# Row 1's statistics ahead of row 0's low halves, kernel halves ahead of signal halves, and the last two convolution rows one by one

## The chip, the core and the metric

One core of a Trainium2 chip runs the whole program. The metric is device time in microseconds, the median of repeated executions. The kernel before takes 1179.39 us, the median of three runs from 1178.54 to 1179.56. Names of engines: PE is TensorE (PEld its weight loads), DVE is VectorE, ACT is ScalarE, POOL is GpSimd, SP is SyncE, which issues most loads. ACT and POOL issue some transfers too.

## The reference, cut to what matters

Four sublayers are computed on x (2048 positions, 576 channels), each with a layer norm in front and a residual sum behind: a Fourier mixing, a gated long convolution, and both again with the same weights.

```python
def _A_ref(x, dft_seq_re, dft_seq_im, dft_hid_re, dft_hid_im):
    a = jnp.einsum("bsd,ed->bse", x, dft_hid_re)
    b = jnp.einsum("bsd,ed->bse", x, dft_hid_im)
    return jnp.einsum("ts,bse->bte", dft_seq_re, a) - jnp.einsum("ts,bse->bte", dft_seq_im, b)

def _B_ref(q, k, v, shift_k, ssm_k, ssm_D):
    k_shift = sum(k_pad[:, t:t + S, :] * shift_k[:, 3 - t] for t in range(4))
    kv = k_shift * v
    y = irfft(rfft(kv, 2S) * rfft(ssm_k, 2S))[:S] + kv * ssm_D     # per channel
    return q * y

x = x + _A_ref(_layernorm(x), ...)
x = x + _B_ref(_layernorm(x), k, v, ...)
x = x + _A_ref(_layernorm(x), ...)
x = x + _B_ref(_layernorm(x), k, v, ...)
```

The signal kv and the kernel ssm_k of the long convolution do not depend on x, so the kernel computes that convolution once and uses it in both gated sublayers.

## The kernel before, in words

**Rows.** Positions are laid out as 128 partitions by 16 rows (J = 16). A row is a 128 x 576 block. Every matrix that PE multiplies is split into a high part, rounded by a copy on ACT (`AF.Copy` into fp32r), and a low part, the difference, taken by DVE. A product is three matmuls: high by high, high by low, low by high. Line 101 is the rounding and line 102 the difference of the general helper `split`.

**The first Fourier sublayer** (`layer`) takes 128 steps, 16 rows for each of two matrices (g) and four column blocks (tb). A step loads a 128 x 512 tile of the sequence matrix (`load_c`, line 171 through SP), splits it (lines 101 and 102, tile `mats<-flts`), and runs 14 matmuls of 512 columns into the accumulators s and rm. In the first 16 steps the row itself must also be made: `load_x`, statistics (`norm_stats`, lines 185 to 187 on DVE, then a power on POOL in line 188), a bias on DVE (194), the normalizing copy on ACT (195), its rounding on ACT (199) and the low halves on DVE (201 for the last 64 channels, 202 for the first 512). From row 8 on the statistics are sums on ACT (652, 654).

**The convolution's branch** (`branch`) is a generator that the steps of `layer` advance in halves, so its work lies between the steps. Its first Fourier stage takes 32 items from the list `todo`: for each row j a kernel half (`src` 1, ssm_k) and a signal half (`src` 0). `f1_loads` keeps three landings ahead. `f1_split` multiplies a signal row with the loaded v (line 430), then rounds (101) and subtracts (102) into tile f1r. `f1_products` issues the small matmuls (PE `bf<-f1r`, six in a visit), copies the two banks out on ACT (455) and stores them (456). Three banks take turns. For the first four rows all kernel halves come first, then the signal halves, and each has its own products of 288 columns; from row 4 on the two halves of a row share a tile pair, and three visits of 384 columns follow when both are there.

**The short convolution** (`convolve`) makes k_shift for the signal rows, two rows at a time: four multiplications (line 397) and three additions (402) of 128 x 1152 elements for each pair on DVE, 56 in all. They are handed out evenly between the halves of the list so that a pair is ready when its first signal half is due (`later`, `left`).

**What sets the order.** The code issues the instructions in one order with priorities; a scheduler places them on each engine's queue, and each engine runs its queue in that order. `behind(...)` (line 105 on) and `tc.issue_after` tell the scheduler to place an instruction no earlier than another one. The stage after this one needs all of `todo` done; it begins at about step 45.

Of the kernel before, what the change touches and what calls it, by code (L numbers as in the profile page):

```python
# [13 lines left out]
OP = mybir.AluOpType  # L14
# [4 lines left out]
D = 576  # L19
J = S // P  # L20
# [5 lines left out]
EPS = 1e-5  # L26
# [5 lines left out]
K_FIRST = 4  # L32
# [22 lines left out]
KR = 4  # L55
# [13 lines left out]
def fnet_h3_kernel(ctx: ExitStack, tc: tile.TileContext, x, c_mat, w_re, w_im, k_pad, v, shift_k,  # L69
                   ssm_k, ssm_d, f1c, i2c, midc, out):  # L70
    nc = tc.nc
# [28 lines left out]
    def split(h, l, src):  # L100
        a = nc.scalar.activation(h, src, AF.Copy).ins  # L101
        return a, nc.vector.tensor_tensor(l, src, h.bitcast(F32), OP.subtract).ins  # L102

    @contextmanager
    def behind(*instructions):
        with ExitStack() as stack:
            for i in instructions:
                stack.enter_context(tc.issue_after(i))
            yield
# [36 lines left out]
    def two(v):  # L146
        return v.rearrange("p (a n) -> p a n", a=2)
# [16 lines left out]

    anchor, made, rounded, pows, biased, halved, added, evac, parted, stored = [], [], [], [], [], [], [], [], [], []

    scaled, asked = [], []

    def load_after(dst, src):
        with tc.issue_after(anchor[-1]):  # L170
# [10 lines left out]
    def norm_stats(src):  # L181
        m = ring["stat"]()
        st, mv, ve, rs = m[:, :12].rearrange("p (a c) -> p a c", a=2), m[:, 12:14], m[:, 14:15], m[:, 15:16]
        for i in range(2):
            nc.vector.bn_stats(st[:, i, :], src[:, i * HD:(i + 1) * HD])
        nc.vector.bn_aggr(mv, st)
        nc.vector.tensor_scalar(ve, mv[:, 1:2], EPS, None, op0=OP.add)  # L187
        pows.append(nc.gpsimd.tensor_tensor(rs, ve, mhalf, OP.pow).ins)  # L188
        return mv, rs, m[:, 16:17]

    def normed(src, y):
        mv, rs, nb = norm_stats(src)
        yield
        biased.append(nc.vector.tensor_scalar(nb, mv[:, 0:1], rs, -1.0, op0=OP.mult, op1=OP.mult).ins)
        scaled.append(nc.scalar.activation(y, src, AF.Identity, bias=nb, scale=rs).ins)

    def to_x(y, j):
        t = xs[:, j, :]
        rounded.append(nc.scalar.activation(t[:, :D], y, AF.Copy).ins)
        h = t.bitcast(F32)  # L200
        nc.vector.tensor_tensor(t[:, D:D + REM], y[:, NC * P:], h[:, NC * P:D], OP.subtract)
        made.append(nc.vector.tensor_tensor(t[:, D + REM:], y[:, :NC * P], h[:, :NC * P], OP.subtract).ins)
        return t

    t_d = dr.tile([P, 2 * J, 2 * D], F32, name="td")
    v_d = [dr.tile([P, 2 * J, HD], F32, name=f"vd{h}") for h in range(2)]
# [7 lines left out]
    X = [None] * J  # L214
# [131 lines left out]
    def parts(i):  # L346
        v = ring[i]()
        return v[:, :D], v[:, D:]
# [4 lines left out]
    def branch():  # L353
# [3 lines left out]
        at = lay(flts, SC_AT + CRAW * NT, ("so", D, 4), ("land", D, 3))  # L357
# [15 lines left out]

        def load_k(upto):
            while k_loaded[0] < min(upto, (J + 4) // 2):
                i = k_loaded[0]
                at = i % KR * 2 * D
                nc.sync.dma_start(ks[:, at:at + 2 * D], k_pad[:, 2 * i * D:2 * (i + 1) * D])
                k_loaded[0] += 1

        def k_rows(row):

            at = row % (2 * KR) * D
            if at + 2 * D <= KR * 2 * D:
                return [(slice(0, 2), two(ks[:, at:at + 2 * D]))]
            return [(slice(n, n + 1), ks[:, o:o + D].unsqueeze(1)) for n, o in ((0, at), (1, 0))]

        def convolve():
            for i in range(J // 2):
                if not wt:  # L390
                    load_w4()
                load_k(i + KR - 1)
                rp = rows[i] = two(ring["rp"]())
                for t in range(4):
                    out_t = two(tmp) if t else rp
                    for n, k in k_rows(2 * i + t):
                        nc.vector.tensor_tensor(out_t[:, n], k, wt[3 - t][:, n], OP.mult)  # L397
                    yield
                    if t == 1:
                        load_k(i + KR)  # L400
                    if t:
                        nc.vector.tensor_tensor(rp, rp, out_t, OP.add)  # L402
                        yield

        todo = [(1, 1), (0, 1)] + [(j, 1) for j in range(2, K_FIRST)] + [(j, 0) for j in range(K_FIRST)]
        todo += [(j, src) for j in range(K_FIRST, J) for src in range(2)]
        loads = [0]

        def f1_loads(upto):
# [16 lines left out]
        def f1_split(j, src):  # L426
            r = landed.pop((j, src))
            if not src:
                row = rows[j // 2][:, j % 2, :]
                nc.vector.tensor_tensor(row, row, r, OP.mult)  # L430
                r = row
            elif j == 0:
                nc.vector.tensor_tensor(r[:1], r[:1], tmp[:1, D:], OP.add)
            if j < K_FIRST:
                xf = parts("xf")
                parted[:] = split(xf[0], xf[1], r)
                return xf
            if not src:
                t = ring["xp"]()
                paired[:] = t[:, :2 * D], t[:, 2 * D:]  # L440
            h, l = (t.rearrange("p (a s d) -> p a s d", a=2, s=2)[:, :, src, :] for t in paired)
            parted[:] = split(h, l, two(r))
            return tuple(paired)
# [14 lines left out]
        conv, made_ops, visits = convolve(), 0, []  # L458
        def visit(half):
            if visits and visits[0][0] <= half:  # L460
                f1_products(*visits.pop(0)[1:])

        for n, (j, src) in enumerate(todo):
            f1_loads(n + 1)
            if n < 2:
                yield
            xf = f1_split(j, src)
            if j < K_FIRST:
                visits += [(2 * n + 2, j, fcs[j], xf, hf * HD, HD, "so", hf * D + src * HD) for hf in range(2)]
            elif src:  # L470
                visits += [(2 * n + 3, j, fcs[j], xf, at, VW, "sp", at) for at in range(0, 2 * D, VW)]
            if n:
                f1_loads(n + 3)
            later = [m for m in range(n + 1, len(todo)) if todo[m][1] == 0 and 7 * (todo[m][0] // 2 + 1) > made_ops]
            for half in range(2):
                visit(2 * n + half)
                if later and n > 2:
                    left = 7 * (todo[later[0]][0] // 2 + 1) - made_ops
                    for _ in range(-(-left // (2 * (later[0] - n) - half)) if left > 0 else 0):
                        next(conv)  # L480
                        made_ops += 1
                yield
# [6 lines left out]
        at = lay(m1, 0, ("df", 2 * D, 3), ("mc", 4 * P, 1))  # L489
# [284 lines left out]
    with tc.issue_after(biased[0]):  # L774
        next(br)
        with behind(*parted, scaled[0]):
            load_c((0, 0, 0))
        load_x(1)
        with behind(rounded[0]):
            load_c((0, 0, 1))  # L780
        load_x(2)
    used = 4
# [17 lines left out]
    for n, whole in layer(get_x0, lambda j: x[:, j, :], done0, pending):  # L800
        part = whole == "part"
        if part:
            whole = False
        if (whole or whole is not None and n % J < J - 1) and n <= F1_END and not part:
            at = n if whole else n - 0.5
# [27 lines left out]
        m = n - PREP  # L833
# [207 lines left out]
    for n, whole in layer(get_x1, lambda j: xb_d[j], done1, pending, 1):  # L1041
# [143 lines left out]
```

## Time and profile before

| what | value |
|---|---|
| median of three runs | 1179.39 us |
| the profiled execution's own time | 1178.94 us |
| its span, first to last instruction | 1177.0 us |
| granted PE clock, mean | 0.999 |
| DVE busy over the span | 867.8 us (74%) |
| ACT busy over the span | 647.8 us (55%) |
| POOL busy over the span | 75.7 us (6%) |

The profile records one execution. The span leaves 1.94 us of its time outside. Busy is the time in which at least one instruction of an engine runs; ends of matmuls are modelled, so a short wait of PE can lie hidden in its busy time. A row of the timeline gives start, duration, engine, line, operation and tiles, and in brackets how long the engine was idle before it and what ended that. SPq, ACTq and POOLq are rows in which an engine's queue issues a transfer.

### The profile page before, as it was taken

Reading aid. Unit: us, or ns where it says so; the run is one execution under the profiler, and the core shown is the slowest. Engines: PE = TensorE matmul, PEld = TensorE weight load, DVE = VectorE, ACT = ScalarE, POOL = GpSimd, SP = SyncE. Lnnn points to the kernel's source line nnn. Section 1 sums busy time; section 2 is a strip of 40 time slices with the busy share of each in tenths; the row PEclk is TensorE's granted clock in tenths of the full one; section 3 lists DMA queues with packets and bytes.
Section 4 is the critical chain, followed back from the end, with each engine's and each line's share of the span. In section 5 each row is a group of like instructions: output and inputs, shape, how many; then the busy total and the mean of one; then the engine's idle time right before and its main releaser. Section 6 shows DMA issues by size and latency. Waiting matters only on the chain.

```text
span 1177.0 us, 18134 instructions
## 1 busy us (share of the span) xinstructions
PE 1165.9 (99%) x6198; PEld 989.8 (84%) x6198; DVE 867.8 (74%) x1564; ACT 647.8 (55%) x1280; POOL 75.7 (6%) x115
## 2 busy tenths in 40 slices
PE   9999999999999999999999999999999999999997
PEld 6776667988899988898888898888888888889997
DVE  7899984688787788877757666866685777774674
ACT  8865655567766667766645667434434445450210
POOL 2310000000000000001101111000000000001111
PEclk9999999999999999999999999999999999999999
DMA  9879898546766766749966777772762877894531
GB/s 326 298 232 306 270 300 284 164 139 178 214 206 192 210 181 191 193 135 258 272 197 216 249 245 239 239 238 89 251 240 73 251 262 257 265 332 149 194 111 41
DMA packets 147453, 255.64 MB, mean 217 GB/s; under 512 B 16161, under 2 KB 56353, under 8 KB 147362
## 3 DMA queue, kind: packets, MB, share of 16 engines
q1 hardware_dynamic: 111890, 210.17, 56.6%
q10 hardware_dynamic: 28560, 37.91, 9.1%
q0 software_dynamic: 6912, 6.43, 2.4%
q8 instruction: 48, 0.79, 0.3%
q14 instruction: 43, 0.35, 0.1%
HBM read 187.80 MB, written 66.65 MB: 216 GB/s over the span
## 4 chain that ended last, share of the span: by engine, by line
PE 93%; DVE 2%; DMA 2%; ACT 1%; issue 1%; SPq 0%; POOL 0%; DVEq 0%; ACTq 0%
PE s L78 54%; PE bk L78 31%; PE rm L78 6%; PE bf L78 2%; DMA t<-ud 1%; DVE f1f L397 1%; DMA vd<-flts 0%; DVE f1f L402 0%; DVE mats L102 0%; DMA early<-in_x 0%; ACT flts L516 0%; DMA flts<-vd 0%; DMA td<-flts 0%; DVE f1r L102 0%; ACT mid L516 0%
## 5 line engine op out<-in xcount | busy, mean ns | idle before, releaser
L78 PE MATMUL s<-mats 128*128 128x512 f32 x2102 | 548.0, 396 | 2.7 <-DVE mats L762 1.5
L78 PEld LDWEIGHTS s<-mats 128*128 128x128 f32 x2102 | 382.7, 189 | 83.8 <-issue 10.9
L102 DVE TENSOR_TENSOR mats<-flts,mats 128x512 fp32r<-128x512 f32 x206 | 140.9, 688 | 55.8 <-ACT mats L101 53.4
L101 ACT ACTIVATE mats<-flts 128x512 fp32r<-128x512 f32 x206 | 128.2, 628 | 79.9 <-PE bk L78 29.6
L516 ACT ACTIVATE flts<-bk 128x288 f32<-128x288 f32 (+1 forms) x192 | 78.4, 409 | 97.7 <-PE bk L78 85.2
L78 PE MATMUL bk<-mid 128*128 128x288 f32 x704 | 127.9, 298 | 0.7 <-DVE mid L522 0.4
L78 PEld LDWEIGHTS bk<-mid 128*128 128x128 f32 x704 | 111.2, 188 | 19.7 <-ACT flts L516 4.5
L78 PE MATMUL bk<-w,u 128*128 128x288 f32 x864 | 120.5, 295 | 0.2
L78 PEld LDWEIGHTS bk<-w,u 128*128 128x128 f32 x864 | 116.8, 188 | 2.4 <-ACT flts L516 1.4
L522 DVE TENSOR_TENSOR mid<-flts,mid 128x576 fp32r<-128x576 f32 (+1 forms) x149 | 92.5, 625 | 7.4 <-ACT mid L516 5.3
L78 PE MATMUL rm<-mats 128*128 128x512 f32 x304 | 94.7, 391 | 0.0
L516 ACT ACTIVATE mid<-flts 128x576 fp32r<-128x576 f32 (+1 forms) x148 | 79.5, 574 | 1.9 <-DMA flts<-vd 0.9
L78 PE MATMUL bk<-mats 128*128 128x288 f32 (+1 forms) x376 | 67.8, 317 | 0.0
L78 PEld LDWEIGHTS rm<-mats 128*128 128x128 f32 x304 | 56.9, 188 | 12.5 <-issue 0.3
L455 ACT ACTIVATE flts<-bf 128x384 f32<-128x384 f32 (+1 forms) x104 | 43.2, 462 | 42.9 <-PE bf L78 40.5
L291 DVE TENSOR_TENSOR flts<-flts,bk 128x288 f32<-128x288 f32 x48 | 21.8, 454 | 60.6 <-PE bk L78 58.3
L78 PE MATMUL s<-t,mats 128*128 128x512 f32 x264 | 65.3, 390 | 0.3 <-DVE t L102 0.3
L188 POOL TENSOR_TENSOR flts<-flts 128x1 f32<-128x1 f32 x34 | 28.0, 824 | 517.0 <-DVE flts L187 517.0
L78 PE MATMUL bk<-mats,t 128*128 128x288 f32 (+1 forms) x368 | 59.3, 303 | 0.0
L78 PEld LDWEIGHTS s<-t,mats 128*128 128x128 f32 x264 | 49.4, 188 | 11.2 <-DVE t L102 0.8
L516 ACT ACTIVATE flts<-flts 64x288 f32<-64x288 f32 x128 | 56.7, 443 | 3.9
L78 PEld LDWEIGHTS bk<-mats 128*128 128x128 f32 x376 | 55.6, 188 | 3.4
(152 smaller groups left out, 1496.6 us busy)
## 6 DMA issues: line engine op xcount, KB each, us to landing
flts<-in_c_mat SPq DMA_DIRECT2D x148, 256.0 KB, 3.5
ph<-in_c_mat SPq DMA_DIRECT2D x54, 512.0 KB, 4.4
flts<-in_c_mat SPq DMA_DIRECT2D x30, 512.0 KB, 5.2
flts<-td SPq DMA_DIRECT2D x53, 288.0 KB, 3.1
td<-flts ACTq DMA_DIRECT2D x36, 384.0 KB, 4.5
vd<-flts ACTq DMA_DIRECT2D x64, 144.0 KB, 3.1
flts<-vd SPq DMA_DIRECT2D x32, 288.0 KB, 4.1
ud<-ph ACTq DMA_DIRECT2D x12, 512.0 KB, 6.4
```

The lines of the kernel that those rows point to most:

```text
L78: return nc.tensor.matmul(ps, lhsT, rhs, start=first, stop=last, skip_group_check=more).ins
L101: a = nc.scalar.activation(h, src, AF.Copy).ins
L102: return a, nc.vector.tensor_tensor(l, src, h.bitcast(F32), OP.subtract).ins
L188: pows.append(nc.gpsimd.tensor_tensor(rs, ve, mhalf, OP.pow).ins)
L291: added[:] = [nc.vector.tensor_tensor(r[:, cs], r[:, cs], ps[:, :HD], OP.add).ins]
L397: nc.vector.tensor_tensor(out_t[:, n], k, wt[3 - t][:, n], OP.mult)
L455: stored[:] = [nc.scalar.activation(so[:, i, :], ps[i], AF.Copy).ins]
L516: last_act.append(nc.scalar.activation(*args, **kw).ins)
L522: nc.vector.tensor_tensor(l, src, h.bitcast(F32), OP.subtract)
```

## The change

Four edits, all in the first 200 us of the program.

1. `to_x` leaves the low halves of row 0 to a new function `low_x`. The start now issues row 1's statistics (`stats0(1)`) first and puts `low_x` of row 0 behind row 1's line 187 (`joined`). The second tile of the sequence matrix is placed behind row 0's low halves as well.
2. The second item of `todo`, the kernel half of row 0, is split behind the last rounding (`rounded[-1:]`), which at that place is row 1's.
3. From row 4 on the list takes the kernel half (1) before the signal half (0). The tile pair is taken at the kernel half, the visits follow the signal half, and the deadlines of the short convolution move with it by one item.
4. The last pair of the short convolution is made one row at a time: 7 operations of 128 x 576 for row 14, then 7 for row 15, each row with its own deadline (`conv_ops`).

```diff
@@ to_x
         rounded.append(nc.scalar.activation(t[:, :D], y, AF.Copy).ins)
+        if j > 0 or X[0] is not None:
+            low_x(y, t)
+        return t
+
+    def low_x(y, t):
         h = t.bitcast(F32)
         nc.vector.tensor_tensor(t[:, D:D + REM], y[:, NC * P:], h[:, NC * P:D], OP.subtract)
         made.append(nc.vector.tensor_tensor(t[:, D + REM:], y[:, :NC * P], h[:, :NC * P], OP.subtract).ins)
-        return t
...
+        def k_row(row, part):
+            at = (row + part.start) % (2 * KR) * D
+            return [(part, ks[:, at:at + D].unsqueeze(1))]
+
@@ convolve
+                for part in (slice(0, 2),) if i < J // 2 - 1 else (slice(0, 1), slice(1, 2)):
...
+        def conv_ops(j):
+            return 7 * (j // 2 + 1) if j < J - 2 else 7 * (J // 2 + j - J + 2)
+
-        todo += [(j, src) for j in range(K_FIRST, J) for src in range(2)]
+        todo += [(j, src) for j in range(K_FIRST, J) for src in (1, 0)]
@@ f1_split
-                parted[:] = split(xf[0], xf[1], r)
+                with behind(*rounded[-1:] if (j, src) == todo[1] else ()):
+                    parted[:] = split(xf[0], xf[1], r)
                 return xf
-            if not src:
+            if src:
                 t = ring["xp"]()
...
-            elif src:
+            elif not src:
                 visits += [(2 * n + 3, j, fcs[j], xf, at, VW, "sp", at) for at in range(0, 2 * D, VW)]
@@ start
         load_x(1)
-        with behind(rounded[0]):
+        stats0(1)
+        with behind(joined[-1]):
+            low_x(LN[0][0], X[0])
+        with behind(rounded[0], made[0]):
             load_c((0, 0, 1))
         load_x(2)
```

Line numbers shift: 195 and 199 stay, 201 and 202 become 206 and 207, 397 and 402 become 406 and 411, 430 becomes 442, 433 becomes 445, 455 and 456 become 468 and 469.

**Start, DVE.** The rows from the low half of the first sequence tile (102) on. flts holds the statistics, early the x rows. Before:

```order
L102 TENSOR_TENSOR mats<-flts,mats 128x512
L201 TENSOR_TENSOR mats<-early,mats 128x64
L202 TENSOR_TENSOR mats<-early,mats 128x512
L102 TENSOR_TENSOR mats<-flts,mats 128x512
L186 BN_AGGR flts<-flts 128x2
L185 BN_STATS flts<-early 128x6
L187 TENSOR_SCALAR flts<-flts 128x1
L433 TENSOR_TENSOR flts<-flts,f1f 1x576
L186 BN_AGGR flts<-flts 128x2
L194 TENSOR_SCALAR flts<-flts 128x1
```

And of the change:

```order
L102 TENSOR_TENSOR mats<-flts,mats 128x512
L186 BN_AGGR flts<-flts 128x2
L185 BN_STATS flts<-early 128x6
L187 TENSOR_SCALAR flts<-flts 128x1
L206 TENSOR_TENSOR mats<-early,mats 128x64
L207 TENSOR_TENSOR mats<-early,mats 128x512
L102 TENSOR_TENSOR mats<-flts,mats 128x512
L186 BN_AGGR flts<-flts 128x2
L194 TENSOR_SCALAR flts<-flts 128x1
```

Row 1's 186 and 187 moved ahead of row 0's low halves and of the second tile's low half; the addition of ssm_d (433, now 445) moved behind row 1's bias (194).

**Start, ACT.** The rows that lead to row 1's rounding (199), from the copies out of the first product's banks on. Before:

```order
L455 ACTIVATE flts<-bf_66 128x288
L455 ACTIVATE flts<-bf_67 128x288
L101 ACTIVATE f1r<-flts 128x576
L456 DMA td<-flts 256x1x288
L455 ACTIVATE flts<-bf_68 128x288
L455 ACTIVATE flts<-bf_66 128x288
L195 ACTIVATE early<-early,flts 128x576
L101 ACTIVATE f1r<-flts 128x576
L199 ACTIVATE mats<-early 128x576
L101 ACTIVATE mats<-flts 128x512
```

And of the change:

```order
L468 ACTIVATE flts<-bf_66 128x288
L468 ACTIVATE flts<-bf_67 128x288
L469 DMA td<-flts 256x1x288
L468 ACTIVATE flts<-bf_68 128x288
L468 ACTIVATE flts<-bf_66 128x288
L195 ACTIVATE early<-early,flts 128x576
L101 ACTIVATE mats<-flts 128x512
L199 ACTIVATE mats<-early 128x576
L101 ACTIVATE f1r<-flts 128x576
```

The kernel halves (f1r) no longer stand in front of row 1; the third sequence tile's rounding (mats<-flts) moved in front of row 1's rounding.

**Between the steps, ACT.** A piece of the queue at about step 27 of the first sublayer; f1r<-f1f is the rounding of a signal half, f1r<-flts that of a kernel half. Before:

```order
L455 ACTIVATE flts<-bf_66 128x384
L101 ACTIVATE f1r<-f1f 128x2x288
L455 ACTIVATE flts<-bf_68 128x384
L101 ACTIVATE mats<-flts 128x512
L456 DMA td<-flts 256x1x384
L455 ACTIVATE flts<-bf_67 128x384
L455 ACTIVATE flts<-bf_68 128x384
```

And of the change:

```order
L468 ACTIVATE flts<-bf_66 128x384
L468 ACTIVATE flts<-bf_68 128x384
L101 ACTIVATE mats<-flts 128x512
L101 ACTIVATE f1r<-f1f 128x2x288
L469 DMA td<-flts 256x1x384
L468 ACTIVATE flts<-bf_67 128x384
L468 ACTIVATE flts<-bf_68 128x384
```

The signal's rounding, which waits for DVE's line 430 (now 442), stood between the two copies that empty a visit's banks; now it stands behind both.

More of the change, by code (lines that the diff above doesn't have):

```diff
@@ L165, in fnet_h3_kernel @@
     anchor, made, rounded, pows, biased, halved, added, evac, parted, stored = [], [], [], [], [], [], [], [], [], []
-    scaled, asked = [], []
+    scaled, asked, joined = [], [], []
     def load_after(dst, src):
@@ L186, in norm_stats @@
         nc.vector.bn_aggr(mv, st)
-        nc.vector.tensor_scalar(ve, mv[:, 1:2], EPS, None, op0=OP.add)
+        joined.append(nc.vector.tensor_scalar(ve, mv[:, 1:2], EPS, None, op0=OP.add).ins)
         pows.append(nc.gpsimd.tensor_tensor(rs, ve, mhalf, OP.pow).ins)
@@ L393, in convolve @@
                 rp = rows[i] = two(ring["rp"]())
[L394 to L402, printed above, removed]
-                        yield
+                for part in (slice(0, 2),) if i < J // 2 - 1 else (slice(0, 1), slice(1, 2)):
+                    for t in range(4):
+                        out_t = two(tmp) if t else rp
+                        for n, k in k_rows(2 * i + t) if part.stop - part.start == 2 else k_row(2 * i + t, part):
+                            nc.vector.tensor_tensor(out_t[:, n], k, wt[3 - t][:, n], OP.mult)
+                        yield
+                        if t == 1:
+                            load_k(i + KR)
+                        if t:
+                            nc.vector.tensor_tensor(rp[:, part], rp[:, part], out_t[:, part], OP.add)
+                            yield
+        def conv_ops(j):
+            return 7 * (j // 2 + 1) if j < J - 2 else 7 * (J // 2 + j - J + 2)
         todo = [(1, 1), (0, 1)] + [(j, 1) for j in range(2, K_FIRST)] + [(j, 0) for j in range(K_FIRST)]
-        todo += [(j, src) for j in range(K_FIRST, J) for src in range(2)]
+        todo += [(j, src) for j in range(K_FIRST, J) for src in (1, 0)]
         loads = [0]
@@ L473, in branch @@
                 f1_loads(n + 3)
-            later = [m for m in range(n + 1, len(todo)) if todo[m][1] == 0 and 7 * (todo[m][0] // 2 + 1) > made_ops]
+            later = [m for m in range(n + 1, len(todo)) if todo[m][1] == 0 and conv_ops(todo[m][0]) > made_ops]
             for half in range(2):
@@ L477, in branch @@
                 if later and n > 2:
-                    left = 7 * (todo[later[0]][0] // 2 + 1) - made_ops
+                    left = conv_ops(todo[later[0]][0]) - made_ops
                     for _ in range(-(-left // (2 * (later[0] - n) - half)) if left > 0 else 0):
```

## The prediction

> **What bounds the kernel now.** I read the page's first part, then the busy times by stretches of the first 195 us, since every edit lies there, then the timeline at the two places where PE stands still.
>
> ```profile
> PE 1165.9 (99%) x6198; PEld 989.8 (84%) x6198; DVE 867.8 (74%) x1564; ACT 647.8 (55%) x1280; POOL 75.7 (6%) x115
> ```
>
> ```profile
> 14.00:60.00 46.00, 45.94 (x218) 35.36 (x219) 40.66 (x98) 41.88 (x87) 12.63 (x12) 1.00 0.88 309
> 60.00:125.00 65.00, 64.56 (x324) 46.15 (x323) 63.86 (x78) 37.04 (x77) 5.76 (x10) 1.00 0.88 274
> 125.00:170.00 45.00, 45.00 (x227) 31.27 (x226) 42.23 (x51) 28.07 (x58) 1.59 (x3) 1.00 0.87 285
> 170.00:195.00 25.00, 25.00 (x129) 17.29 (x127) 9.74 (x14) 13.36 (x28) 0.00 (x0) 1.00 0.84 269
> ```
>
> A row of the second fence gives the stretch, its length, then the busy time of PE, PEld, DVE, ACT and POOL. PE is idle for 1177.0 - 1165.9 = 11.1 us of the whole span, and from 14 to 195 us for only 0.50 us. So PE's own work bounds the kernel, and the change leaves that work as it is. DVE is full from 60 to 125 us (63.86 of 65) and ACT nearly so from 14 to 60 (41.88 of 46), but they hold PE only for moments. A gain has to come out of PE's few gaps; a loss has to be a new gap. The largest gap that the change touches is at the start:
>
> ```profile
> 8.71 0.22 DVE L201 TENSOR_TENSOR mats<-early,mats 128x64 fp32r<-128x64 f32 x1
> 8.84 0.68 DVE L202 TENSOR_TENSOR mats<-early,mats 128x512 fp32r<-128x512 f32 x1
> 9.75 0.66 PE L78 MATMUL bf<-f1r 64*128 64x288 f32 x6 [0.18 <-ACT flts L455]
> 10.05 0.20 DVE L186 BATCH_NORM_AGGREGATE flts<-flts 128x2 f32<-128x12 f32 x1
> 10.34 2.11 PE L78 MATMUL s<-mats 128*128 128x512 f32 x8
> 10.49 0.13 DVE L187 TENSOR_SCALAR flts<-flts 128x1 f32<-128x1 f32 x1
> 10.54 0.74 DVE L433 TENSOR_TENSOR flts<-flts,f1f 1x576 f32<-1x576 f32 x1
> 10.72 1.00 POOL L188 TENSOR_TENSOR flts<-flts 128x1 f32<-128x1 f32 x1 [4.57 <-DVE flts L187]
> 11.24 0.71 ACT L455 ACTIVATE flts<-bf 128x288 f32<-128x288 f32 x2
> 11.75 0.21 DVE L194 TENSOR_SCALAR flts<-flts 128x1 f32<-128x1 f32 x1 [0.35 <-POOL flts L188]
> 12.00 0.87 ACT L195 ACTIVATE early<-early,flts 128x576 f32<-128x576 f32 x1
> 12.77 0.67 ACT L101 ACTIVATE f1r<-flts 128x576 fp32r<-128x576 f32 x1
> 13.34 0.67 ACT L199 ACTIVATE mats<-early 128x576 fp32r<-128x576 f32 x1
> 14.06 3.06 PE L78 MATMUL s<-mats 128*128 128x512 f32 x12 [1.16 <-ACT mats L199]
> ```
>
> PE ends step 0 and stands for 1.16 us until row 1 is rounded at 14.0. Behind that wait lies one chain: DVE 187 (10.49), POOL's power (10.72 to 11.72), DVE 194, ACT 195, ACT 199. It starts late because DVE makes row 0's low halves and a tile's low half first.
>
> **Row 1's statistics in front.** I place the new DVE order with the old spacings. What stands ahead stays, so the first row in its new place, 186, comes where 201 started, at 8.71. From 186 to 187 it was 0.44 us (10.05 to 10.49), so 187 comes at 9.15, 1.34 us earlier. Then row 0's low halves: 206 at 9.20, 207 at 9.33, done at 10.01. PE needs them at 10.34 (the eight matmuls), since it is in a product visit until then: this move costs PE nothing, and would cost at most 10.01 - 9.52 = 0.49 us if that visit did not cover it. The second tile's low half (102, as long as 202) then runs from 9.94 to 10.62 and is first needed in step 1, after 13 us.
>
> The power starts 0.23 us after 187, at 9.38. How long it takes, the trace shows both ways:
>
> ```profile
> 4.95 0.55 POOL L188 TENSOR_TENSOR flts<-flts 128x1 f32<-128x1 f32 x1 [4.50 <-DVE flts L187]
> 41.15 4.20 POOL L656 TENSOR_TENSOR flts<-flts 128x1 f32<-128x1 f32 x1 [2.98 <-DVE flts L655]
> ```
>
> 0.55 us at its shortest, 4.20 at its longest, and 1.00 at 10.72, where it ended 0.44 us after 433, the long DVE operation beside it. In the new order 206, 207 and 102 stand right behind 187. So it ends at 9.93 if nothing holds it, or at 10.62 + 0.44 = 11.06 if all three do. It cannot be held longer: behind 102 and one 186 DVE comes to 194, which waits for it. The Trainium skill, GPSIMD Engine Reference, section Key points, speaks against this place: GpSimd shares its SBUF interfaces with VectorE and contends with instructions that have two SBUF inputs. By that rule the late end holds, which the three rows agree with; without it the early one would.
>
> 194 follows at 10.7 to 11.1 and lets ACT go 0.25 us later (11.75 to 12.00), at 10.95 to 11.35. ACT itself is free when it has copied out the second visit: PE's visit ends at 10.41, two copies take 0.71, so 11.15. ACT 195 thus starts between 11.15 and 11.35 instead of 12.00. From there to PE it took 2.06 us (12.00 to 14.06) with one rounding of 0.67 between 195 and 199. Now a rounding of a sequence tile lies there, about as long. So PE starts step 1 at 13.2 to 13.4: **0.65 to 0.85 us earlier**, and I take 0.75. It cannot be more than about 1.3, the gap itself with the end of the matmuls in it.
>
> That tile must have landed. Its load was issued at 7.01 and took 6.0:
>
> ```profile
> 7.01 0.33 SPq L171 DMA_DIRECT2D flts<-in_c_mat  x1
> flts<-in_c_mat SPq DMA_DIRECT2D x1, 256.0 KB, 6.0
> 10.00:20.00 10.00, 8.84 (x42) 6.82 (x41) 9.65 (x34) 9.14 (x16) 4.83 (x7) 1.00 1.08 364
> ```
>
> On SP one x row is now ahead of it where two x rows and a kernel half were, 576 KB less, at 364 GB/s some 1.6 us. So 13.0 becomes 11.4, before ACT comes to it at about 12.0. If it still landed at 13.0, 199 would start at 13.7 and PE at 14.4, a loss of 0.35: the lower end.
>
> Two things queue behind the moved pieces. Row 0's kernel half is split some 0.6 us later and its POOL load of f1c goes out behind the second power, at 9.9 to 11.1 instead of 5.46:
>
> ```profile
> 5.46 0.69 POOL L175 DMA_DIRECT2D f1r<-in_f1c  x1
> f1r<-in_f1c POOLq DMA_DIRECT2D x3, 128.0 KB, 6.6
> 20.69 0.67 PE L78 MATMUL bf<-f1r 64*128 64x288 f32 x6
> ```
>
> With 6.6 us it lands by 17.7, and the first visit that reads it comes at 20.69 less the gain, 19.9. Two microseconds of cover: I cost it at nothing.
>
> **Does the start's gain last?** Only if the helpers follow. PE's order of the next steps is the same, and DVE's and ACT's work up to 60 us is the same in sum, with 5.3 and 4.1 us idle. The tightest place I find is step 13:
>
> ```profile
> 58.25 0.69 DVE L102 TENSOR_TENSOR mats<-flts,mats 128x512 fp32r<-128x512 f32 x1
> 58.35 2.89 PE L78 MATMUL s<-mats 128*128 128x512 f32 x12
> ```
>
> The low half of its tile ends at 58.94, after PE began the step at 58.35. PE did not wait since its order puts four high-by-high matmuls first, 4 x 2.89/12 = 0.96 us, so it needed the low half at 59.31: 0.37 to spare. If DVE comes there no earlier than now, 0.38 of the 0.75 is given back and 0.37 stays; if it comes 0.4 earlier, all stays. I take 0.5. Below 60 us the whole can be lost if DVE is later than now.
>
> **The convolution's order.** Kernel halves need no short convolution, so moving them first and letting each deadline slip by one of 32 items lightens DVE ahead of most products. What that can return are these waits:
>
> ```profile
> 108.87 1.66 PE L78 MATMUL s<-mats 128*128 128x512 f32 x6
> 110.67 0.79 PE L78 MATMUL bf<-f1r 64*128 64x384 f32 x6
> 118.28 1.66 PE L78 MATMUL s<-mats 128*128 128x512 f32 x6
> 118.35 0.74 DVE L430 TENSOR_TENSOR f1f<-f1f,flts 128x576 f32<-128x576 f32 x1
> 119.13 0.69 ACT L101 ACTIVATE f1r<-f1f 128x576 fp32r<-128x576 f32 x1 [0.25 <-DVE f1f L430]
> 119.72 0.47 ACT L455 ACTIVATE flts<-bf 128x384 f32<-128x384 f32 x1
> 120.24 0.79 PE L78 MATMUL bf<-f1r 64*128 64x384 f32 x6 [0.30 <-ACT flts L455]
> 127.87 1.66 PE L78 MATMUL s<-mats 128*128 128x512 f32 x6
> 129.46 0.79 PE L78 MATMUL bf<-f1r 64*128 64x384 f32 x6
> ```
>
> Six matmuls and the change to a visit take 1.59 us when nothing waits (127.87 to 129.46). At 110.67 it was 1.80 and at 120.24 1.96: 0.21 and 0.37 lost, 0.58 together. At 120.24 a bank's copy stood on ACT behind a signal's rounding that waited for DVE 430; in the new queue that rounding stands behind both copies. I take 0.35 of the 0.58.
>
> The last pair row by row turns seven DVE operations of 1152 into fourteen of 576:
>
> ```profile
> 83.80 2.68 DVE L397 TENSOR_TENSOR f1f<-f1f 128x576 f32<-128x576 f32 x3
> L397 DVE TENSOR_TENSOR f1f<-f1f x36: 744/1346/1359, 30.2 to 164.1; 128x1152 f32<-128x1152 f32 x28, 128x576 f32<-128x576 f32 x8
> ```
>
> Two halves cost 0.744 + 0.67 = 1.41 against 1.346, 0.07 more; one operation of the pair was split already, so six times, 0.4 us. It now ends later, between 165 and 185 us, where DVE is busy 9.74 of 25 us: hidden. Uncovered it would be 0.4.
>
> **Sum**, against the profiled 1178.94 us: - 0.5 - 0.35 = - 0.85, so 1178.1. The median of the runs is 0.45 above the profiled time, so I predict **1178.5 us**. My case's own range, from 0.3 to 1.9 us gained, is 1177.5 to 1179.1.
>
> **Rivals.** *The gain is given back* (no change, 1179.3). The stretch 60 to 125 us is DVE's pace: PE comes 0.5 earlier and waits there 0.5 longer. For it: 63.86 of 65 busy. Against: from 125 on PE does not wait at all, so DVE is behind for short whiles only, and the new order eases just that stretch.
>
> *Slower: the signal half is now the last thing before a visit.* The chain short convolution, 442, ACT's rounding, DVE's 102 used to end one item ahead of the visits; now nothing lies between. If DVE is one operation (1.27 to 1.35) late at a row, PE stands for that long; twelve rows could do so. It decides from the third late row: 3 x 1.3 - 0.5 = +3.4, 1182.8. For it: DVE is full and these operations are long. Against: the split's place in the code stays three half-items ahead of the first visit, and DVE has less to do before most of them.
>
> *Clearly faster.* PE's busy time may hide waits, its ends being modelled. By its rows, from 60 to 125 us a matmul took 64.56/324 = 0.199 and from 125 to 170 45.00/227 = 0.198, so less than 0.5 us is hidden; with the whole start gap (1.3) and both waits (0.58), 2.4 us, 1177.0. The Trainium skill's first page (Trainium Kernel Development and Optimization, Best Practices) would judge by the busy weight loads instead. By that rule 71% from 60 to 125 us against the page's 84% means 10 us to win, an estimate, about 1169. Here it does not hold: the share is as low, 69%, from 125 to 170 where PE never waits.
>
> **How the numbers follow.** Forecast 0.65; given back 0.17; slower by that chain or another 0.12; clearly faster 0.06. A difference under 0.2% (2.4 us) cannot be told from none here. The forecast, the return and a third of the slower case lie within it: 0.86 the same. Slower by more 0.08, faster by more 0.06. The range goes from 1177.0, the whole of PE's gaps, to 1180.4, where PE loses one long DVE operation (1.35) and keeps 0.35 at the start; beyond lies about 0.13.
>
> **What would show it.** In the changed profile: the power of row 1 starts near 9.4 and ends by 11.1; PE's second run of twelve matmuls starts at 13.2 to 13.4 with less than 0.6 us of wait in front; the wait of 0.30 at the visit near 120 is gone; PE idle falls from 11.1 to about 10 us. It is wrong if ACT waits for the tile in front of 199, if products wait for DVE 102 of a signal half, or if PE's new lead is gone by step 13.

## The result: slower, and the profile after

| | before | after |
|---|---|---|
| median | 1179.39 us (six runs, 1178.39 to 1180.01) | 1184.26 us (six runs, 1180.89 to 1185.01) |
| profiled execution, its time and span | 1178.94 / 1177.0 us | 1180.89 / 1178.7 us |

The ratio over the single runs is 1.0037, with a 95% interval from 1.0024 to 1.005 (the two medians give 1.0041). The prediction was 1178.5 us, range 1177.0 to 1180.4, with 0.08 for slower by more than 2.4 us: it was wrong in sign and in size. The profiled execution of the changed kernel is also the quickest of its six, so its trace shows the smaller part of the loss.

The page's busy times, and the busy times by stretches (start:end, length, then PE, PEld, DVE, ACT, POOL, the granted PE clock, DMA share, GB/s), after:

```profile
PE 1166.0 (99%) x6198; PEld 989.7 (84%) x6198; DVE 869.1 (74%) x1570; ACT 646.5 (55%) x1280; POOL 76.3 (6%) x115
```

```profile
14.00:60.00 46.00, 45.03 (x213) 34.02 (x212) 39.83 (x95) 40.48 (x84) 12.47 (x11) 1.00 0.87 310
60.00:125.00 65.00, 62.95 (x315) 45.41 (x314) 62.16 (x77) 36.24 (x76) 5.23 (x9) 1.00 0.84 267
```

PE's work is the same. It stands for 0.97 us between 14 and 60 us (0.06 before) and for 2.05 us between 60 and 125 us (0.44 before). The timeline has three places. First the start, which went as planned:

```profile
9.17 0.14 DVE L187 TENSOR_SCALAR flts<-flts 128x1 f32<-128x1 f32 x1
9.38 1.07 POOL L188 TENSOR_TENSOR flts<-flts 128x1 f32<-128x1 f32 x1 [3.86 <-DVE flts L187]
11.41 0.87 ACT L195 ACTIVATE early<-early,flts 128x576 f32<-128x576 f32 x1
12.17 0.63 ACT L101 ACTIVATE mats<-flts 128x512 fp32r<-128x512 f32 x1
13.42 3.02 PE L78 MATMUL s<-mats 128*128 128x512 f32 x12 [0.39 <-ACT mats L199]
...
50.14 0.96 PE L78 MATMUL s<-mats 128*128 128x512 f32 x3
51.07 0.68 DVE L102 TENSOR_TENSOR mats<-flts,mats 128x512 fp32r<-128x512 f32 x1
51.81 2.35 PE L78 MATMUL s<-mats 128*128 128x512 f32 x9 [0.72 <-DVE mats L102]
54.87 1.91 PE L78 MATMUL s<-mats 128*128 128x512 f32 x6 [0.25 <-ACT mats L199]
...
80.25 0.74 DVE L442 TENSOR_TENSOR f1f<-f1f,flts 128x576 f32<-128x576 f32 x1
81.02 0.33 SPq L434 DMA_DIRECT2D flts<-in_ssm_k  x1
86.16 0.68 ACT L101 ACTIVATE f1r<-flts 128x576 fp32r<-128x576 f32 x1 [3.61 <-DMA flts<-in_ssm_k]
86.75 0.69 ACT L468 ACTIVATE flts<-bf 128x288 f32<-128x288 f32 x2
87.50 0.66 PE L78 MATMUL bf<-f1r 64*128 64x288 f32 x6 [2.05 <-ACT flts L468]
89.36 2.89 PE L78 MATMUL s<-mats 128*128 128x512 f32 x12
```

Step 1 began at 13.42 instead of 14.06. At step 11 (the second group) the lead was gone: PE waited for the low half of the step's tile. At 87.5 us (the third) a new wait stands, the largest of the stage. ACT stood for 3.61 us with the rounding of a kernel half (`f1r<-flts`) whose load was still under way, and the copies (468) that empty a product visit's banks stood behind it. PE's next visit needed those banks.

Why was the load late? Three landings (the buffers that the loads fill) take turns, so the landing came free only when DVE had multiplied row 3's signal half (442, at 80.25). SP issued the load at 81.02, and it landed about 5 us later, near 86.1. And why did ACT come to it so early? A kernel half needs no short convolution, and the new list names it one item earlier. The scheduler put row 5's kernel half ahead of row 4's signal half, which waits for DVE, and ahead of two visits' copies. This is ACT's queue of the changed kernel at that place:

```
L101 ACTIVATE f1r<-f1f 128x576
L101 ACTIVATE mats<-flts 128x512
L469 DMA td<-flts 256x1x288
L101 ACTIVATE f1r<-flts 128x2x288
L468 ACTIVATE flts<-bf_68 128x288
L468 ACTIVATE flts<-bf_67 128x288
L469 DMA td<-flts 256x1x288
L468 ACTIVATE flts<-bf_67 128x288
L468 ACTIVATE flts<-bf_66 128x288
L101 ACTIVATE mats<-flts 128x512 x2
L469 DMA td<-flts 256x1x288
L101 ACTIVATE f1r<-f1f 128x2x288
```

The first row is row 3's signal half, the fourth row 5's kernel half, the last row 4's signal half. Before, ACT stood for row 5's kernel half too (first row below), but later than row 4's signal half and with nothing behind it that PE waited for. With row 7's kernel half (second row) the kernel before already did in small what the change did here:

```profile
92.12 0.69 ACT L101 ACTIVATE f1r<-flts 128x576 fp32r<-128x576 f32 x1 [2.37 <-DMA flts<-in_ssm_k]
109.06 0.69 ACT L101 ACTIVATE f1r<-flts 128x576 fp32r<-128x576 f32 x1 [2.37 <-DMA flts<-in_ssm_k]
109.74 0.87 ACT L455 ACTIVATE flts<-bf 128x384 f32<-128x384 f32 x2
110.66 0.47 PEld L78 LDWEIGHTS bf<-f1r 64*128 64x128 f32 x6 [0.56 <-ACT flts L455]
```

Two copies stood behind that rounding, and the visit at 110.67 waited for them. This is the 0.21 us that the prediction found lost there and hoped to win back by lightening DVE.

### The profile page after: what moved, and what is told of

The parts are those of the page before. It is cut to its first block, busy times and chain, and to the rows that moved or that the text cites. A ratio compares the mean times of both kernels' runs of the same rounds, so it can differ in the third digit from the quotient of the medians.

```text
span 1178.7 us, 18145 instructions
## 1 busy us (share of the span) xinstructions
PE 1166.0 (99%) x6198; PEld 989.7 (84%) x6198; DVE 869.1 (74%) x1570; ACT 646.5 (55%) x1280; POOL 76.3 (6%) x115
## 4 chain that ended last, share of the span: by engine, by line
PE 92%; DMA 3%; DVE 2%; ACT 1%; issue 1%; POOL 0%; SPq 0%; ACTq 0%; DVEq 0%
PE s L78 53%; PE bk L78 31%; PE rm L78 6%; PE bf L78 2%; DMA flts<-in_v 1%; DMA flts<-in_c_mat 1%; DVE mats L102 1%; DMA vd<-flts 1%; POOL flts L669 0%; DMA early<-in_x 0%; ACT flts L529 0%; DMA flts<-vd 0%; DVE mats L207 0%; DVE f1r L102 0%; DVE flts L185 0%
```

## The experiments

Four kernels first: each part of the change alone, and the change once more. Beside them the kernel before ran at 1179.41 us (27 runs). Beside the three later groups it ran at 1178.81, 1179.21 and 1178.73 us, so a time is to be held against the kernel before of its own group; the ratios are.

**The start alone** (edits 1 and 2).

> Edits 1 and 2 alone (row 1's statistics in front, row 0's kernel half split behind row 1's rounding), the rest as before. Theory: the start's 0.65 us is won, and given back around step 11 (50 to 55 us), where the low half of a tile came 0.93 us later than before because the loads of the kernel halves of rows 2 and 3 were pushed behind others; 0.9 and 0.4 us were lost there in the changed kernel's profile, 0.65 won. So 1179.4 + 0.2 to + 0.7, that is 1179.6 to 1180.1. Rival: those lost pieces come from the other edits (the list's new order begins at row 4, its loads a little earlier), then the 0.65 stay and the time is 1178.7. A third: most of the changed kernel's 4.9 us come from here, 1182 or more.

Measured: 1179.17 us, ratio 1.0002 (0.9993 to 1.001). The timeline of this kernel:

```profile
13.29 3.02 PE L78 MATMUL s<-mats 128*128 128x512 f32 x12 [0.42 <-ACT mats L199]
50.01 0.96 PE L78 MATMUL s<-mats 128*128 128x512 f32 x3
50.39 0.68 DVE L102 TENSOR_TENSOR mats<-flts,mats 128x512 fp32r<-128x512 f32 x1
51.13 2.34 PE L78 MATMUL s<-mats 128*128 128x512 f32 x9 [0.17 <-DVE flts L658]
58.57 2.88 PE L78 MATMUL s<-mats 128*128 128x512 f32 x12
```

and the same places before:

```profile
50.14 0.68 DVE L102 TENSOR_TENSOR mats<-flts,mats 128x512 fp32r<-128x512 f32 x1
50.83 3.00 PE L78 MATMUL s<-mats 128*128 128x512 f32 x12
```

PE comes to step 1 0.77 us earlier and to step 11 0.82 earlier, but the low half comes 0.25 later (50.39 against 50.14). Step 13 starts at 58.57 against 58.35. The whole gain is given back in steps 11 and 12, and 0.2 us on top. The trace takes the theory's side; the time itself, 1179.17, lies between the theory's range and the rival's 1178.7.

**The list's order alone** (edit 3).

> Edit 3 alone (from row 4 on the kernel half before the signal half), the rest as before. Theory: ACT stands for a kernel half's load in front of the copies that empty a visit's banks, and PE waits for these copies, 2.2 us in the changed kernel's profile at 87.5 us and more in the runs that were not profiled; the waits of before at 110 and 120 us (0.58) go. So the profile shows PE waiting some 2 us for ACT's copies behind a rounding that waits for a load, and the time is 1181 to 1184. Rival: the wait at 87.5 us needs the start's shifted loads too; then no such wait shows, and the time is 1178.8 to 1179.4.

Measured: 1182.81 us, ratio 1.003 (1.0019 to 1.004). The theory held. Timeline and stretches of this kernel:

```profile
85.53 0.68 ACT L101 ACTIVATE f1r<-flts 128x576 fp32r<-128x576 f32 x1 [3.76 <-DMA flts<-in_ssm_k]
86.87 1.06 PE L78 MATMUL bf<-f1r 64*128 64x288 f32 x6 [2.24 <-ACT flts L455]
```

```profile
83.52:86.94 3.42, 1.18 (x6) 0.64 (x6) 3.42 (x5) 1.28 (x3) 0.00 (x0) 1.00 0.94 311
86.94:90.35 3.41, 3.41 (x12) 2.65 (x13) 2.74 (x4) 1.61 (x4) 0.53 (x1) 0.50 0.47 144
```

Here is a second cost that nobody had on the list. As PE resumes, the granted clock (third number from the end) falls to 0.50 and stays there for 3.41 us. The six small matmuls of the visit take 1.06 us instead of 0.66. 3.41 us at half speed are 1.7 us lost. The sum 2.24 + 1.7 - 0.58 (the returned waits) = 3.4 us is what was measured, 1182.81 - 1179.41; in this trace itself PE fell 3.1 us further behind the kernel before from step 13 to 200 us.

**The last two rows alone** (edit 4).

> Edit 4 alone (the last two convolution rows made one by one), the rest as before. Theory: hidden, 1179.4 within 0.5. Rival: it moves DVE's operations in the stretch before 165 us so that a signal half comes late, 1181 or more.

Measured: 1179.03 us, ratio 0.9997 (0.9988 to 1.0005). Hidden, as expected.

**The change once more.**

> The changed kernel once more. Its profiled execution took 1180.89 and the median of its runs 1184.26. Theory: what differs from execution to execution is how long the loads of the kernel halves take to land where ACT waits for them in front of a visit's copies (3.61 us of ACT, 2.05 of PE in the profile seen). A profile of an execution near 1184 then shows PE waiting for ACT's copies 5 to 6 us in all between 60 and 170 us, behind such loads. Rival: the 3.4 us lie behind 200 us or in a lower granted clock, with the waits before 170 us as seen.

Measured: 1183.9 us, ratio 1.0033 (1.0021 to 1.0045); the profiled execution took 1184.79. Timeline and stretches of that execution:

```profile
8.01 0.73 PE L78 MATMUL s<-mats 128*128 128x512 f32 x2 [0.57 <-ACT mats L199]
9.22 0.74 PE L78 MATMUL s<-mats 128*128 128x512 f32 x2 [0.48 <-DVE mats L102]
11.45 0.67 PE L78 MATMUL bf<-f1r 64*128 64x288 f32 x6 [1.49 <-ACT flts L468]
12.04 3.66 PE L78 MATMUL s<-mats 128*128 128x512 f32 x8
88.20 0.68 ACT L101 ACTIVATE f1r<-flts 128x576 fp32r<-128x576 f32 x1 [4.11 <-DMA flts<-in_ssm_k]
89.54 0.67 PE L78 MATMUL bf<-f1r 64*128 64x288 f32 x6 [2.57 <-ACT flts L468]
91.96 3.93 PE L78 MATMUL s<-mats 128*128 128x512 f32 x12
```

```profile
87.29:90.70 3.41, 1.16 (x8) 0.92 (x9) 3.41 (x4) 1.74 (x5) 0.17 (x1) 1.00 0.58 204
90.70:94.12 3.42, 3.42 (x10) 2.64 (x9) 2.79 (x6) 2.08 (x4) 0.36 (x1) 0.50 0.76 213
```

Neither theory held whole. The wait is the same one and 0.52 us longer (2.57 against 2.05), since the load landed later; the 5 to 6 us of the theory did not come. Behind it the clock is halved for 3.41 us, which costs 1.7 us, the rival's lower clock: twelve matmuls take 3.93 us where they took 2.89 in the first profile. Nothing lies behind 200 us. The start of this execution also had a wait of 1.49 us and half clock behind it (eight matmuls in 3.66 us instead of 2.11), because a sequence tile landed late. The kernel before has the same queue on ACT at that place, and in the eight other profiles with the start's edits step 1 began between 13.0 and 13.5 us, where here it was 16.02. So I do not count that to the change, though two profiles of the changed kernel cannot show how often it comes. Of the 5.9 us that this execution lay behind the kernel before at 200 us, 2.0 came from that start, 0.4 up to step 13 and 4.1 from the wait with its half clock; 0.58 were returned.

Then the cure, in the first of four kernels beside which the kernel before ran at 1178.81 us (35 runs). One line keeps a kernel half from row 4 on behind the signal half ahead of it in the list:

```diff
             h, l = (t.rearrange("p (a s d) -> p a s d", a=2, s=2)[:, :, src, :] for t in paired)
-            parted[:] = split(h, l, two(r))
+            with behind(*parted if src else ()):
+                parted[:] = split(h, l, two(r))
```

**The list's order alone, with that placement.**

> Edit 3 alone as in the run before, but each kernel half from row 4 on is placed behind the signal half in front of it in the list, so that it is no longer pulled ahead of copies out of the banks while its load is under way. Theory: ACT then finds row 5's kernel half landed (issued near 80, landed near 85.5, needed near 91), PE's wait of 2.2 us at 87 and the 3.4 us of half clock behind it (1.7 us) are gone, and with the 0.58 us returned at 110 and 120 us the time is 1178.8 to 1179.4. Rival: the list's new order costs by itself (deadlines one item later, landings freed later); then a wait of over 1 us appears elsewhere between 60 and 170 us, 1181 or more.

Measured: 1177.99 us, ratio 0.9992 (0.9983 to 1.0); the theory held, and the time came out a little below its range. Timeline and stretch of this kernel:

```profile
81.93 0.69 ACT L101 ACTIVATE f1r<-flts 128x576 fp32r<-128x576 f32 x1
91.34 0.67 ACT L101 ACTIVATE f1r<-flts 128x576 fp32r<-128x576 f32 x1
132.71 0.79 PE L78 MATMUL bf<-f1r 64*128 64x384 f32 x6 [0.77 <-ACT flts L456]
```

```profile
60.00:125.00 65.00, 65.00 (x327) 46.82 (x326) 63.33 (x79) 37.55 (x80) 5.74 (x10) 1.00 0.86 275
```

From 60 us on no kernel half's load is waited for: row 4's is rounded at 81.93, row 5's at 91.34. From 60 to 125 us PE never stands, so the waits near 110 and 120 us are gone as well. The new order as such costs nothing that shows. What cost was where one rounding stood in ACT's queue: + 3.4 us without the placement and - 0.8 with it, each against the kernel before of its own group, 4.2 us together. A wait of 0.77 us is left at 132.7.

**The whole change with that placement.**

> The changed kernel with the same one placement added, nothing else. Theory: almost all of its loss goes, 1179.0 to 1179.7 (the start's gain is still given back between 50 and 60 us). Rival: the other edits, together with this one, cost 1 us or more of their own (the start in the run of 1184.79 had a wait of 1.5 us and 3.4 us of half clock), 1180.5 or more.

Measured: 1178.46 us, ratio 1.0 (0.9991 to 1.001). The theory's side: the loss is gone. Its profile still shows the start's gain given back, and more than that. Step 13 began at 59.93 us, 1.6 later than before. ACT had stood for 2.19 us, up to 17.6 us, for row 2's kernel half:

```profile
17.60 0.69 ACT L101 ACTIVATE f1r<-flts 128x576 fp32r<-128x576 f32 x1 [2.19 <-DMA flts<-in_ssm_k]
```

**The change without the list's order.** Edit 3 alone undone.

> The changed kernel with edit 3 alone undone: start, row 0's kernel half behind row 1, last two rows one by one. Theory: the parts add up, + 0.0 (start, measured 1179.17) and - 0.2 (single rows, 1179.03): 1178.6 to 1179.4, no wait for a kernel half in front of copies. Rival: start and single rows cost something only together, 1181 or more.

Measured: 1179.35 us, ratio 1.0004 (0.9996 to 1.0012). The parts add up to nothing measurable.

**The start, with row 8's statistics on DVE** (the number from which rows use sums on ACT goes from 8 to 9).

> Edits 1 and 2 alone, and row 8's statistics made by DVE like those of rows 0 to 7 instead of by two sums on ACT. Theory: the start's gain is given back because ACT, without a gap from 17 to 31 us, brings the helpers of steps 5 to 11 no earlier; ACT has two long passes less (0.7 and 0.8 us), the low half of step 11's tile ends some 0.5 to 1 us before 51.08, and PE's lead of 0.8 us outlives step 12 at least in part: 1178.3 to 1178.9, step 13 begins before 58.2. Rival: DVE is the limit there; then the low half of step 11 ends at 51.1 or later, and step 13 begins at 58.4 or later, 1179.2 or more.

Measured: 1178.97 us, ratio 0.9997 (0.9989 to 1.0006). The low half of step 11 came 0.76 us earlier than with the start alone (49.63 against 50.39), and PE no longer waited there. It then waited 0.44 us in step 12 for a row's low half:

```profile
49.63 0.68 DVE L102 TENSOR_TENSOR mats<-flts,mats 128x512 fp32r<-128x512 f32 x1
54.60 1.21 PE L78 MATMUL s<-mats 128*128 128x512 f32 x4 [0.44 <-DVE mats L207]
58.28 1.08 PE L78 MATMUL s<-mats 128*128 128x512 f32 x4
```

Step 13 at 58.28 lies between the two theories: 0.29 us better than with the start alone, but only level with before (58.35). The limit had moved on to the next helper. Against the kernel before of its group the time is + 0.2 us, so no gain that can be measured.

**The best of the parts**, beside the kernel before at 1179.21 us (21 runs).

> Edits 3 and 4 with the placement of the kernel halves behind the signal halves; no edit at the start. Theory: the placement's gain (measured 0.8 us, 0.9992 of the kernel before) and the single rows' (0.4 us measured, not sure) add up: 0.6 to 1.3 us below the kernel before of the same call, no wait over 1 us between 60 and 170 us. Rival: a signal half late near 131 us (a wait of 0.77 us in the run before) moves or grows with the other conv order, no gain.

Measured: 1177.91 us, ratio 0.999 (0.9982 to 0.9999), the only kernel whose interval lies wholly below the kernel before. It does so by a hair and is the best of the kernels tried, so part of its 1.3 us may be chance. PE stands for 0.12 us from 60 to 170 us:

```profile
60.00:125.00 65.00, 65.00 (x326) 46.78 (x325) 63.83 (x78) 37.44 (x78) 5.74 (x10) 1.00 0.88 279
125.00:170.00 45.00, 44.88 (x226) 31.16 (x226) 39.07 (x52) 26.83 (x56) 1.58 (x3) 1.00 0.86 281
```

**All parts with row 8's statistics on DVE.**

> All four edits, the placement, and row 8's statistics on DVE. Theory: the start's 0.7 us outlives step 12 by 0.1 to 0.5 us as with the statistics alone, and the rest as in the run above: 0.8 to 1.6 us below the kernel before of the same call. Rival: DVE, with 1.3 us more of work ahead of step 13, is late there and the start's gain is lost as before: equal to or slower than the run above.

Measured: 1178.6 us, ratio 0.9996 (0.9987 to 1.0005). That is 0.6 us below the kernel before, where the theory had 0.8 to 1.6, and no better than the run without the start's edits. The rival fits: step 13 began at 58.84 us, so the start's lead was gone again.

**Row 2's kernel half rounded later.** The last two kernels (kernel before: 1178.73 us, 20 runs) were aimed at the start's loss, with PE's order unchanged:

```diff
-                with behind(*rounded[-1:] if (j, src) == todo[1] else ()):
+                with behind(*rounded[-1:] if (j, src) == todo[1] else rounded[3:4] if (j, src) in todo[2:4] else ()):
```

> Edits 1 and 2 alone, and row 2's kernel half rounded one row later on ACT (behind row 3's rounding), where its load has landed; PE's order is unchanged. Theory: the start's gain is lost between 16 and 52 us because the start pushed that load from 4.87 to 11 us while its rounding moved ahead, so that ACT, which has no gap there, stands for it (0.56 us in the first run of the start, 1.11 in the changed kernel, 2.19 in the run with the placement, where step 13 began at 58.57, 59.25 and 59.93). Without the wait the low half of step 11's tile ends near 50.5 instead of 51.08 and step 13 begins at 57.7 to 58.2: 0.4 to 0.8 us faster than the start alone, 0.9993 to 0.9999 of the kernel before. Rival: ACT's work alone sets the pace; then step 13 begins at 58.4 or later.

Measured: 1179.14 us, ratio 1.0006 (0.9996 to 1.0015). The theory fell. ACT no longer stood for the kernel half, but at 16.77 us it stood 1.17 us for a row of x instead, and step 13 began at 58.68:

```profile
16.77 0.87 ACT L195 ACTIVATE early<-early,flts 128x576 f32<-128x576 f32 x1 [1.17 <-DMA early<-in_x]
58.68 1.52 PE L78 MATMUL s<-mats 128*128 128x512 f32 x6
```

```profile
16.00:31.00 15.00, 15.00 (x72) 11.42 (x70) 12.93 (x39) 14.20 (x28) 3.44 (x5) 1.00 1.05 394
```

The second fence is this kernel's stretch from 16 to 31 us: the DMA share is 1.05, so the times of the transfers add up to more than all 16 transfer engines have. When one load was no longer waited for, another one was. That the transfers set the helpers' pace there is read from these rows; no run took transfers away, so it is not shown.

**The whole change with both placements.**

> All four edits, the placement of the kernel halves from row 4 on, and the same later rounding of row 2's kernel half. Theory: step 13 begins at 57.7 to 58.3, not 59.93, and PE waits nowhere over 1 us between 14 and 170 us: 1.0 to 1.9 us below the kernel before of the same call. Rival: the start's gain is lost again by another wait before step 13: no better than without the start edits (0.999).

Measured: 1178.23 us, ratio 0.9993 (0.9984 to 1.0002). Step 13 began at 58.77, and 0.5 us is what the time gained: the rival again. The start's edits add nothing measurable to the others.

## Why the prediction was wrong, point by point

- **The start's new order: right.** 187 at 9.17 (predicted 9.15), the power 1.07 us long and ended at 10.45 (bounds 9.93 and 11.06), ACT 195 at 11.41 (bounds 11.15 and 11.35, so 0.06 past them), PE at 13.42 (13.2 to 13.4) with 0.39 us of wait in front (below 0.6). The power was held, but not by all three DVE operations: it ended 0.41 us after 207 (done at 10.04), while 102 still ran. The gain was 0.64 us in this profile and 0.77 with the start alone; I took 0.75. ACT did not wait for the tile ahead of 199.
- **"Does the start's gain last": wrong, this is the first step that failed.** I kept 0.5. With the start's edits as they are, step 13 began 0.0 to 1.6 us later than before in every profile (2.4 in the execution whose first tiles were late). Two faults: I named step 13 as the tightest place, but step 11 was tighter. There the low half ended at 50.82 (50.14 + 0.68) and PE's first use of it came after one matmul of the step begun at 50.83, so at about 51.06: 0.24 us to spare against 0.37. (PE's order there changed too, which I had taken to be the same: three matmuls of step 11 now run ahead of the first use, as the row of three at 50.14 shows, and that was not enough.) And I argued that the helpers' work is the same in sum, with idle time to spare, over 14 to 60 us. That idle time lies late. From 16 to 31 us ACT was busy for 14.62 of 15 us before:

```profile
16.00:31.00 15.00, 15.00 (x72) 11.69 (x71) 13.09 (x39) 14.62 (x28) 2.36 (x5) 1.00 1.01 353
```

- **"Two things queue behind the moved pieces": one was missed.** The load of f1c was counted, and rightly at nothing. But SP's queue changed as well: row 2's kernel half, loaded at 4.87 us before, was issued at 11.04. ACT then stood for it for 1.11 us in the changed kernel's profile, 0.56 with the start alone, 2.19 with the placement; the low half of step 11's tile began at 51.07, 50.39 and 51.77, and step 13 at 59.25, 58.57 and 59.93. I had moved it past other loads to make room for a sequence tile and never asked who reads it. Rounding it later took this wait away and not the loss, so what the lead would need in order to last stays open.
- **The short convolution's order: right as to the gain, partly by another path.** The waits near 110 and 120 us went in every kernel with edit 3, 0.55 to 0.58 us where I took 0.35. The 0.21 us near 110 had come by way of row 7's kernel half, rounded in front of copies while its load was under way. With the placement PE stands nowhere from 60 to 125 us.
- **The slower rival: right sign, wrong mechanism.** It had the signal half late on DVE in front of a visit, from the third late row on. What came was the kernel half, late by DMA, once, with copies out of the banks behind it on ACT. The step that failed is the reading of the queue: I took the list's order for ACT's order. The row that should have warned me was in the profile before: ACT stood 2.37 us for a kernel half near 92 us, and again near 109 us, there with copies behind it that PE waited for. I asked what a rounding in front of copies costs only for the one rounding that moved behind them.
- **The price of a wait: too small.** Rivals and range took a wait at its own length. The half clock behind it added 1.7 us to 2.24 or 2.57 and nothing to 2.05; the last section says why.
- **The last pair row by row: right.** Its 0.4 us of DVE is hidden: with edit 4 alone PE's first matmul behind 200 us came 0.02 us from where it was before.
- **The clearly faster rival** by the share of weight loads is refuted: with PE never idle from 60 to 125 us, weight loads are busy 46.78 of 65 us, 72%, and the kernel is about 1 us faster, not 10.

Measured against the sum: - 0.5 at the start was 0.0 to + 1.6 in the profiles (+ 2.4 in one); - 0.35 was - 0.58; and + 2.05 to + 2.57 of waiting, mostly with + 1.7 of clock, were not in it. In the first profile 0.9 - 0.58 + 2.05 = 2.4 us, and PE lay 2.3 us behind at 200 us (0.9 is 59.25 - 58.35 at step 13). With the wait and clock of the execution of 1184.79 it is 0.9 - 0.58 + 2.57 + 1.7 = 4.6 us, beside 4.9 and 4.5 measured; that sum is put together from two executions, so its fit is in part luck. I have two profiles of the changed kernel, so the share of each cause over all its runs stays open.

## What to carry to other kernels

When an operation is named earlier and depends on little but a load, a scheduler can place it well ahead of its neighbours in the list. Look for it in the new queue, and ask whether that load is there by then, and what stands behind it on its engine. An operation that waits for a load should stand behind the copies that free the accumulators of the bottleneck engine; here one such placement was worth 4.2 us.

A lead won early on the bottleneck engine lasts only as far as its helpers and their loads come earlier too. Check every later step's spare time, and the busy share of helpers and DMA in the stretch right behind, not over the whole stage.

## What the runs showed of the hardware

A pause of PE can cost more than its length. Waits of 2.24 and 2.57 us were followed by 3.41 us at a granted clock of 0.50, and so was the start where waits of 0.48 and 1.49 us came close together. The wait of 2.05 us in the changed kernel's first profile was not.

The traces show what decides. In all 14 profiles the granted clock changes only at whole multiples of 3.413 us behind its first rise. With edit 3 alone it rises at 5.02 us, falls at 86.94 (24 multiples later) and rises again at 90.35. So each trace can be cut into stretches of that length, and PE's idle time can be added up in each. These are such stretches of the changed kernel, first around the wait of 2.05 us in the first profile, then at the start of the execution of 1184.79:

```profile
82.65:86.07 3.42, 2.79 (x15) 1.61 (x13) 3.42 (x5) 0.00 (x0) 0.00 (x0) 1.00 1.06 354
86.07:89.48 3.41, 1.98 (x12) 1.60 (x13) 3.31 (x5) 2.57 (x7) 0.53 (x1) 1.00 0.64 221
```

```profile
8.78:12.20 3.42, 1.49 (x9) 0.89 (x10) 2.69 (x11) 1.23 (x3) 1.71 (x2) 1.00 0.91 309
12.20:15.61 3.41, 3.41 (x9) 2.64 (x10) 2.95 (x10) 3.22 (x7) 2.66 (x4) 0.50 0.98 305
```

The wait of 2.05 us lay across an edge, so 0.6 us of it fell into one stretch and 1.4 into the next, and the clock stayed at 1.00. At the start 1.93 us of idle time, in two pieces, fell into one stretch, and the next one ran at 0.50; the waits of 2.24 and 2.57 us left 2.24 and 2.25 us in one. Over all profiles, each of the 17 stretches at full clock with 1.93 us or more of idle time was followed by half clock (14 of them at the end of a program), and none with 1.73 us or less. So it is neither one wait's length alone nor its moment alone, but the idle time within such a stretch, and whether a wait of some 2 us costs 1.7 us more is partly luck.

The Trainium skill, TensorE: Matmul & The Clock Gate, section What's actually happening, describes a monitor that halves the clock after an idle window of about 3.4 us and restores it after a busy one as long. The 3.4 us at half speed agree; the idle time does not, since 1.93 us within such a stretch were enough here, so gaps well below 3 us have to be counted as dangerous.
